# Folding the output parts with one float32 copy and float32 identity matmuls

## The chip, the cores and the metric

The kernel runs on one core of a Trainium2 chip. The metric is the device time of one execution in microseconds, as the median of several runs: 925.74 us before the change (4 runs, 923.92 to 926.63).

## The reference

Two attention layers over the same 2048 tokens of width 512 are computed and mixed by a gate. With g = sigmoid(sum of x * gate_w), the output is g * A + (1 - g) * B.

- A is a recurrent memory transformer with 32 heads of width 128. The tokens come in 64 segments of 32. To each segment 8 memory rows are put in front; q, k and v are projections of these 40 rows, masked softmax attention follows, then the output projection Wo. The first 8 rows of that output are the memory of the next segment, the other 32 are its output rows:

```python
for s in range(n_seg):
    h = concatenate([mem, xs])            # 8 + 32 rows
    ...                                   # q, k, v, softmax, o
    o = einsum('bhte,hed->btd', o, Wo)
    mem = o[:, :M]                        # needed by segment s + 1
    outs.append(o[:, M:])
```

- B is an infini-attention layer with 32 heads of width 16 in 4 blocks of 512 tokens, with a causal mask inside the block and a linear memory over the blocks. It depends on nothing in A.

So the 64 segments of A form a chain: no projection of segment s + 1 can be finished before the Wo product of segment s has become its memory.

## The kernel before

All work is planned in Python as a list of operations for each engine, in a fixed order. A class `Prog` derives the waits from what each operation reads and writes (named resources such as "WH0", and PSUM banks), and `Banks` hands out the eight PSUM banks; which bank an operation gets, and so which earlier reader it must wait for, follows from the order in which banks were given back.

In the first 80 us or so B's projections run and the weights are loaded. Then `plan_a` runs the 64 segments. One segment is a string of units in the order that the list `A_ORDER` (L912) gives, four strings for the four segments of a group. `Q0x` to `V1y` are the projections, `S`, `X`, `M`, `L`, `N` scores and softmax, `PV`, `PL` the product with V, `E` the copies out of PSUM, `W0a` to `W1b` the product with Wo. Between them stand slots for other work: `bS`, `bE`, `bP` for attention B's scores, exponential and product (a share per segment, so that they end around segment 57), `Fc`, `Ff`, `Fe` for fills: projections for the last 8 rows of the coming group's segments (`left_units`), the Wo product of the group's last 8 rows (`ol_units`) and the final mix (`tail_units`).

TensorE is used in four groups of 32 columns: a segment has only 32 rows in the main pass (8 memory rows and 24 of its tokens; the other 8 are handled for four segments at once in the left units), and so each of the four groups takes a part of the heads. For the Wo product this means that a PSUM bank holds, in its four partition strips of 32, four partial sums of the same 32 output rows. They have to be added over the strips and transposed. This is what the fold does: a matmul whose stationary operand is a 128x32 piece of the partial sums and whose moving operand is `fold`, four 32x32 identities on top of each other (128x32), gives the transposed sum.

The partial sums are float32 and the matmul is bf16, so each half (`hf`, 256 columns) of the bank is first split into two bf16 terms:

- H0, H1 (`part_hi`, L1047): copy of the half to `WH` in bf16, on VectorE (DVE).
- l0, l1 (`part_lo`, L1051): `WL` = PSUM - `WH`, in bf16, on DVE. The second gives the PSUM bank back.
- F0, F1 (`fold`, L1058): 16 matmuls each, for two column blocks, two terms (WH and WL accumulate into the same output) and four strips.
- hm0, hm1 copy the first 8 columns, the new memory, to `hT` on ScalarE (ACT); the next segment's Q0x waits for hm0 and Q0y for hm1. ax0, ax1 copy the other 24 to `aT_st` on DVE.

The same two steps and fold serve the Wo product of a group's last rows in `ol_units`, with `LN_sb[:, 0]` and `LN_sb[:, 1]` as the two terms and ACT for the copy. There both halves share one resource name, so that the second copy waits for the first subtraction. For the last group the matmuls are issued in segment 63, and the copies, subtractions and folds come in the final loop (L1453) after the tail units' Wo product of B and its copy `t1` (L1139).

The attention B chain (L867 to L899) turns a bank with a DVE transpose into `oTt` (16 blocks of 32 columns, of which 0 to 15 hold the numerator and 16 the denominator), and writes the reciprocal to `rden`.

Of the kernel before, what the change touches and what calls it, by code (L numbers as in the profile page):

```python
# [5 lines left out]
ALU = mybir.AluOpType  # L6
AX = mybir.AxisListType
BF16 = mybir.dt.bfloat16
F32 = mybir.dt.float32
# [218 lines left out]
def build(nc, es, A_x, A_mem0, A_Wq, A_Wk, A_Wv, A_Wo, B_wq, B_wk, B_wv, B_wo, B_beta, gate_w, out, dbg=None):  # L228
    v = NS()
# [30 lines left out]
    def alloc(stack, *specs):  # L260
        at, spans = 0, {}
        for name, shape, dt, n in specs:
# [14 lines left out]
          ("gBp", [128, 8], F32, 0), ("omgBp", [128, 8], F32, 0),  # L277
          ("onesb", [128, 128], BF16, 0), ("mneg", [128, 224], BF16, 0),
          ("pQj", [128, 512], BF16, 0), ("MZj", [128, 2, 84], BF16, 0), ("PT", [128, 2, 512], BF16, 2), ("orow", [128, 16, 2, 16], BF16, 0),
          ("rden", [128, 16], F32, 0), ("adot", [128, 16, 16], F32, 0),  # L280
          ("oTs", [128, 512], BF16, 0), ("oTg", [128, C, 128], BF16, 0),
          ("KTj", [128, 512], BF16, 2), ("QTj", [128, 512], BF16, 0), ("Vj", [128, 4, 2, 84], BF16, 0),
          ("aTg", [128, C, 128], BF16, 0), ("fold", [128, SEG], BF16, 0), ("VTL", [128, 4, H // 2, 8, 2], BF16, 0),
          ("WH", [128, DM], BF16, 0), ("WL", [128, DM], BF16, 0))
    esP = ExitStack()
    in_p = alloc(esP, ("wkB", [128, C, DM], BF16, 0), ("wqB", [128, C, DM], BF16, 0), ("phK", [128, 4, DM], BF16, 0), ("etmp", [128, 512], BF16, 5),
          ("bmask", [128, 136], BF16, 0), ("mskT", [128, 2, 2, 8, 2], BF16, 0), ("mem0_sb", [128, DM], BF16, 0), ("gwr_sb", [128, 128], BF16, 0), ("beta_sb", [128, HB], BF16, 0),
# [180 lines left out]

def plan_warm(v):
    P, Rs, BK = v.P, v.Rs, v.BK  # L470
    P.op("dve", lambda d: d.memset(v.WH[:, :], 0.0), writes=[Rs("warm")], name="warm0")
    bk = BK.take()

    def f(pe):
        ins = None
        for n in range(WARM):
            ins = pe.matmul(v.pb[bk], v.WH[:, 0:128], v.WH[:, :], start=True, stop=True)
        return ins
    P.op("pe", f, reads=[Rs("warm")], writes=[v.rbank[bk]], name="warm")
    BK.give(bk)  # L480
# [263 lines left out]
class BAttn:  # L744
# [134 lines left out]

    def memory(self, job, G):  # L880
        v, P, Rs = self.v, self.v.P, self.v.Rs
        sb, f = job // 4, job % 4
        nm = "%d_%d%d" % (sb, f, G)
        nb = v.BK.take()

        def fn(pe):
            ins = None
            for j in range(4):
                ins = pe.matmul(v.pb[nb][32 * j:32 * j + 32, :], v.MZj[:, G, 17 * j:17 * j + 32], v.pQj[:, :], start=True, stop=True)
            return ins  # L890
# [3 lines left out]
        rm, rr, rt = v.rden[:, :], Rs("rden"), Rs("oTt")  # L894
# [17 lines left out]
A_ORDER = [o.split() for o in (  # L912
    """
    bT Q0x bE Q0y q0 TQ0 K0x K0y k0 TK0 Q1x bP Q1y q1 K1x TQ1 K1y k1 S0 bS V1x TK1 X0 M0 V0x V0y S1 Ff v0 bE V1y L0 X1 n0 N0 M1 Fe L1 Fc
    PV0 PL0 Fc n1 v1 N1 E0a E0b PV1 PL1 E1a W0a W0b E1b W1a Fe W1b Ff Fe bP H0 bS Fc l0 F0 bP bE hm0 H1 l1 ax0 Fe Ff Fe bS F1 hm1 oL bE
    ax1""",
    """
    Q0x Q0y q0 K0x K0y Q1x k0 Q1y TQ0 TK0 q1 K1x TQ1 K1y S0 X0 V0x V0y k1 M0 V1x TK1 L0 S1 V1y v0 X1 M1 N0 v1 n0 L1 n1 N1 Fc Ff PV0 PL0
    E0b E0a bT Fe Fc PV1 PL1 E1b W0a E1a Fe W0b W1b W1a H0 bP l0 bS H1 Fc F0 bE Ff l1 bP bS hm0 F1 hm1 ax0 oL Fe ax1 bE""",
    """  # L920
    bT Q0x Q0y q0 bP K0x K0y TQ0 k0 TK0 Q1x Q1y K1x K1y S0 q1 bS X0 TQ1 k1 V0x V0y M0 V1x TK1 bE v0 S1 L0 V1y N0 X1 M1 bP n0 L1 PV0 v1 n1
    N1 PL0 E0b PV1 E0a PL1 E1a bP E1b oL bT W0a W0b W1a W1b H0 Fc bS l0 Fc Ff H1 Fe bE l1 Fc F0 Ff Fc F1 hm0 ax0 Fe hm1 ax1 bS bP Fe bE""",
    """
    Q0x Q0y bT q0 K0x K0y k0 TQ0 TK0 Q1x Q1y q1 K1x TQ1 bS K1y S0 bP V0x V0y bE X0 k1 M0 TK1 V1x L0 S1 n0 X1 v0 V1y M1 bP N0 L1 PV0 v1 PL0
    E0b N1 PV1 n1 PL1 E0a bT E1b W0a W0b W1b E1a W1a H0 Ff l0 Fe bS H1 bE oL Ff l1 bS Fe Ff F0 hm0 ax0 Fe F1 hm1 ax1""")]
# [5 lines left out]
def plan_a(v, nseg):  # L931
# [98 lines left out]
        return units  # L1030

    HD = 128 * C // 2
    w_res = (("WH0", "WH1"), ("WL0", "WL1"))
    o_res = (("LN0", "LN0"), ("LN1", "LN1"))

    def out_part(bk, ks, first, lhs, reads, name):

# [6 lines left out]
            return ins  # L1044
        P.op("pe", f, reads=reads + [Rs("Wo%d" % k) for k in sorted({k // 2 for k in ks})], writes=[rbank[bk]], name=name)

    def part_hi(bk, hf, hi, res, name, eng="act"):  # L1047
        c = slice(HD * hf, HD * (hf + 1))
        evac(eng, hi[:, c], pb[bk][:, c], [bk], [Rs(res[0][hf])], "%sh%d" % (name, hf))

    def part_lo(bk, hf, hi, lo, res, name):  # L1051
        c = slice(HD * hf, HD * (hf + 1))
        P.op("dve", lambda d: d.tensor_tensor(lo[:, c], pb[bk][:, c], hi[:, c], ALU.subtract),  # L1053
             reads=[rbank[bk], Rs(res[0][hf])], writes=[Rs(res[1][hf])], name="%sl%d" % (name, hf))
        if hf:
            B.give(bk)

    def fold(bk, hf, hi, lo, res, name):  # L1058

        def f(pe):  # L1060
            ins = None
            for n in range(2):
                for m, t in enumerate((hi, lo)):
                    for j in range(4):
                        o = 256 * hf + 128 * n + SEG * j
                        ins = pe.matmul(pb[bk][SEG * j:SEG * (j + 1), SEG * n:SEG * (n + 1)], t[:, o:o + SEG], v.fold[:, :],  # L1066
                                        start=(m == 0), stop=(m == 1), skip_group_check=True)
# [6 lines left out]
    def ol_units(g):  # L1074
# [5 lines left out]
        for b in range(2):  # L1080
            def u(b=b):
                if b == 0:
                    st["bk"] = B.take()
                out_part(st["bk"], range(4 * b, 4 * b + 4), b == 0, lambda h: OTL[par][:, h, :], [Rs("OTL%d" % par)], "ol%d_%d" % (g, b))
                if b == 1:
                    return u2

            def u2():
                for hf in range(2):
                    part_hi(st["bk"], hf, LN_sb[:, 0, :], o_res, "olev%d" % g)  # L1090
                    part_lo(st["bk"], hf, LN_sb[:, 0, :], LN_sb[:, 1, :], o_res, "olev%d" % g)
            units.append(("c", u, "ol%d_%d" % (g, b)))

        def ut():
            bks = [B.take(), B.take()]
            for hf in range(2):
                fold(bks[hf], hf, LN_sb[:, 0, :], LN_sb[:, 1, :], o_res, "olf%d" % g)
            return lambda: ut2(bks)

        def ut2(bks):  # L1100
# [72 lines left out]
    def segment(s, fill):  # L1173
# [138 lines left out]

        def w_fold(hf):
            wb["f%d" % hf] = B.take()
            fold(wb["f%d" % hf], hf, v.WH, v.WL, w_res, "wf%d" % s)

        def w_mem(hf):
            if s + 1 == nseg:
# [45 lines left out]
        for b in range(2):  # L1364
# [62 lines left out]
    for g in range(ngrp):  # L1427
# [62 lines left out]
```

## Time and profile before

| what | value |
|---|---|
| median of 4 runs | 925.74 us (923.92 to 926.63) |
| the profiled execution | 923.92 us; its span 922.2 us |
| PE (TensorE matmul) busy | 855.2 us, 93% |
| PEld (weight loads) busy | 442.1 us, 48% |
| DVE busy | 651.5 us, 71% |
| ACT busy | 589.2 us, 64% |
| POOL busy | 246.4 us, 27% |
| granted TensorE clock | 0.998 |
| WH copies (DVE, 128) | 53.7 us, 420 ns each |
| WL subtractions (DVE, 128) | 54.4 us, 425 ns each |
| LN subtractions (DVE, 32) | 13.6 us, 425 ns each |

The span runs from the first to the last instruction of the core. Busy times are sums of the records of an engine; a matmul's record includes the time that its data take through the array, so neighbouring records overlap. A row of the groups reads: line, engine, operation, what is written and read, partitions x elements and type, how often; then busy time and mean duration of one; then how long the engine was idle just before such instructions and which instruction ended the idle time. In the chain of work that ended last, each piece has its start and its length, and then the engine, tile and line.

### The profile page before, as it was taken

What the parts mean: (1) busy time and instruction counts of PE and PEld (TensorE: products, weight loads), DVE (VectorE), ACT (ScalarE), POOL (GpSimd) and SP (SyncE); (2) the same over time, 40 slices, a digit from 0 to 9 for tenths busy, and PEclk for the clock granted to TensorE, in tenths of its full rate; (3) what the DMA queues carried; (4) which work ended last, traced back from release to release, by engine and by line L of the source; (5) the groups of instructions that cost most, each with busy time, mean ns of one, the idle gap of its engine ahead of it and who ended that gap; (6) DMA issues with size and microseconds to landing.
All of it is one profiled execution on the core that took longest, in us unless ns stands there. A gap on an engine that the chain in (4) does not pass through costs nothing. (4 is left out here: it accounts for less than half of the span.)

```text
span 922.2 us, 51467 instructions
## 1 busy us (share of the span) xinstructions
PE 855.2 (93%) x23054; PEld 442.1 (48%) x23054; DVE 651.5 (71%) x1507; ACT 589.2 (64%) x1284; POOL 246.4 (27%) x556
## 2 busy tenths in 40 slices
PE   8998989998999999998999999999999989999886
PEld 4544444444444454544454555444444445444443
DVE  3856657776676868677777778777677776868654
ACT  5755666666666666666666666666666666666443
POOL 3601222222222322222233232313222232222110
PEclk9999999999999999999999999999999999999999
DMA  9995000000001111101011111100011111000010
GB/s 324 405 384 188 13 12 17 24 12 24 17 22 43 22 39 33 34 15 27 13 26 38 22 46 32 29 14 22 22 33 38 39 29 38 17 21 5 26 44 20
DMA packets 63957, 51.36 MB, mean 56 GB/s; under 512 B 34288, under 2 KB 60152, under 8 KB 62200
## 3 DMA queue, kind: packets, MB, share of 16 engines
q1 hardware_dynamic: 62008, 35.48, 13.8%
q10 hardware_dynamic: 1728, 12.58, 3.3%
q8 instruction: 181, 2.97, 1.3%
q14 instruction: 40, 0.33, 0.1%
HBM read 33.47 MB, written 14.57 MB: 52 GB/s over the span
## 5 line engine op out<-in xcount | busy, mean ns | idle before, releaser
L816 ACT ACTIVATE PT<-ps 128x1024 bf16<-128x1024 f32 x160 | 163.2, 1020 | 33.9 <-PE ps L802 32.9
L823 POOL TENSOR_SCALAR_AFFINE_SELECT PT<-PT 128x512 bf16<-128x512 bf16 (+1 forms) x96 | 75.5, 787 | 266.5 <-ACT PT L816 256.2
L964 PE MATMUL ps<-Wv_sb,hT 128*32 128x512 bf16 x2048 | 139.3, 379 | 0.0
L964 PE MATMUL ps<-Wq_sb,hT 128*32 128x512 bf16 x2048 | 136.2, 380 | 1.3 <-ACT hT L357 0.8
L964 PE MATMUL ps<-Wk_sb,hT 128*32 128x512 bf16 x2048 | 135.4, 379 | 0.0
L1042 PE MATMUL ps<-Wo_sb,OT_sb 128*32 128x512 bf16 x2048 | 122.3, 380 | 1.3 <-DMA Wo_sb<-in_A_Wo_dram 1.3
L1266 POOL TENSOR_TENSOR P_sb<-P_sb,R_sb 128x64 bf16<-128x64 bf16 x128 | 53.5, 418 | 237.6 <-PE ps L1220 132.7
L357 ACT ACTIVATE OT_sb<-ps 128x320 bf16<-128x320 f32 x192 | 76.7, 434 | 52.3 <-PE ps L1288 38.5
L359 DVE CAST V_sb<-ps 128x512 bf16<-128x512 f32 x128 | 87.7, 685 | 23.9 <-PE ps L964 19.6
L976 DVE STREAM_TRANSPOSE QT_sb<-QN_sb 128x256 f32<-128x256 f32 x128 | 56.3, 440 | 50.9 <-ACT QN_sb L357 50.7
L357 ACT ACTIVATE QN_sb<-ps 128x512 bf16<-128x512 f32 x128 | 77.1, 602 | 21.8 <-PE ps L964 19.0
L964 PEld LDWEIGHTS ps<-Wk_sb,hT 128*32 128x32 bf16 x2048 | 54.0, 97 | 52.7 <-issue 2.3
L359 DVE CAST WH<-ps 128x256 bf16<-128x256 f32 x128 | 53.7, 420 | 33.0 <-PE ps L1042 31.1
L1042 PEld LDWEIGHTS ps<-Wo_sb,OT_sb 128*32 128x32 bf16 x2048 | 50.2, 96 | 46.0 <-issue 1.8
L1229 ACT ACTIVATE P_sb<-ps 128x224 bf16<-128x224 f32 x128 | 45.6, 357 | 40.9 <-PE ps L1220 17.6
L964 PEld LDWEIGHTS ps<-Wq_sb,hT 128*32 128x32 bf16 x2048 | 47.9, 96 | 47.8 <-ACT hT L357 15.3
L976 DVE STREAM_TRANSPOSE KT_sb<-KN_sb 128x256 f32<-128x256 f32 x128 | 56.1, 438 | 15.4 <-ACT KN_sb L357 13.0
L1253 ACT ACTIVATE R_sb<-ps 128x160 f32<-128x160 f32 x128 | 38.9, 304 | 40.4 <-PE ps L1246 40.4
L802 PE MATMUL ps<-QTj,KTj 32*128 32x256 bf16 (+1 forms) x768 | 62.3, 254 | 1.5 <-ACT aT_st L357 1.5
L1260 DVE TENSOR_TENSOR P_sb<-P_sb,R_sb 128x160 bf16<-128x160 bf16 x128 | 42.5, 332 | 29.3 <-ACT R_sb L1256 17.9
L1276 PE MATMUL ps<-P_sb,V_sb 32*128 32x40 bf16 x2048 | 35.3, 178 | 29.9 <-DVE P_sb L1260 13.3
L357 ACT ACTIVATE LN_sb<-ps 128x512 bf16<-128x512 f32 (+1 forms) x96 | 50.5, 526 | 11.8 <-DVE LN_sb L1053 8.8
(136 smaller groups left out, 1549.9 us busy)
## 6 DMA issues: line engine op xcount, KB each, us to landing
Wk_sb<-in_A_Wk_dram ACTq DMA_DIRECT2D x4, 1024.0 KB, 8.4
scr_kqd<-stgk SPq DMA_DIRECT2D x16, 256.0 KB, 8.7
Wq_sb<-in_A_Wq_dram ACTq DMA_DIRECT2D x4, 1024.0 KB, 7.4
Wv_sb<-in_A_Wv_dram ACTq DMA_DIRECT2D x4, 1024.0 KB, 7.5
Wo_sb<-in_A_Wo_dram SPq DMA_DIRECT2D x8, 512.0 KB, 6.8
scr_vd<-V SPq DMA_DIRECT2D x16, 136.0 KB, 6.7
Vj<-scr_vd SPq DMA_DIRECT2D x32, 68.0 KB, 2.4
Wo_sb<-in_A_x_dram SPq DMA_DIRECT2D x8, 256.0 KB, 7.5
```

The costliest lines, as they stand in the source:

```text
L357: P.op("act", lambda a: a.activation(dst, src, ACT.Copy), reads=[v.rbank[k] for k in bks], writes=dres, name=name)
L359: P.op("dve", lambda d: d.tensor_copy(dst, src), reads=[v.rbank[k] for k in bks], writes=dres, name=name)
L802: ins = pe.matmul(v.pb[bks[x]][:, 256 * e + o:256 * e + o + w], KT[e][r, 128 * kc:128 * (kc + 1)], QT[r, q0:q0 + w], start=True, stop=True ...
L816: P.op("act", lambda a: a.activation(pt[:, :, :], v.ps[:, bks[0]:bks[1] + 1, :], ACT.Exp, scale=v.SCALE_B), reads=[v.rbank[b] for b in bks ...
L823: P.op("gp", lambda g: g.affine_select(mv, mv, [[0, mv.shape[1]], [1, 128]], ALU.is_ge, 0.0, base=0, channel_multiplier=-1), reads=[rp], w ...
L964: ins = pe.matmul(pb[bk][SEG * j:SEG * (j + 1), :], lhs(c), cols(w, j) if split else w[:, 512 * j:512 * (j + 1)], start=(c == 0), stop=(c ...
L976: P.op("dve", lambda d: d.transpose(to, src), reads=reads, writes=writes, name=name)
L1042: ins = pe.matmul(pb[bk][SEG * j:SEG * (j + 1), :], lhs(4 * k + j), Wo_sb[:, 4 * k + j, :], start=(first and k == ks[0]), stop=False, skip ...
L1229: P.op("act", lambda a: a.activation(P_sb[:, b, :], pb[bk][:, 0:224], ACT.Exp, scale=SCALE), reads=[rbank[bk]], writes=[Rs("P%d" % b), Rs( ...
L1253: P.op("act", lambda a: a.activation(R_sb[:, b, :], pb[bk][:, 224:384], ACT.Ln), reads=[rbank[bk]], writes=[Rs("R%d" % b)], name="ln%d_%d" ...
L1260: P.op("dve", lambda d: d.tensor_tensor(wide(P_sb, b)[:, :, 0:L], wide(P_sb, b)[:, :, 0:L], R_sb[:, b, :].rearrange("p (i q) -> p i q", q= ...
L1266: P.op(ENG["n"], lambda d: d.tensor_tensor(left(P_sb), left(P_sb), grp04(R_sb[:, b, :]), ALU.mult), reads=[Rs("R%d" % b)], writes=[Rs("P%d ...
```

## The change

The two bf16 terms become one float32 copy, and the fold multiplies it by a float32 `fold` constant: 8 matmuls for each half, each writing its output once, in place of 16 that accumulate in pairs. `part_lo` and the units l0 and l1 disappear. `WF` (float32, 512 columns) takes the room of `WH` and `WL`; in the ol part the two bf16 rows of `LN_sb` are seen as one float32 row, and each half has its own resource. The PSUM bank is given back after the second copy. To make room for the larger `fold`, `rden` goes: the reciprocals are written to the unused column 17 of `oTt`. The copies of the last group's ol part are planned right after the last segment, ahead of the final loop. The matmuls that run at the start to warm TensorE read a bf16 view of `WF`.

```diff
-          ("rden", [128, 16], F32, 0), ("adot", [128, 16, 16], F32, 0),
+          ("adot", [128, 16, 16], F32, 0),
...
-          ("aTg", [128, C, 128], BF16, 0), ("fold", [128, SEG], BF16, 0), ("VTL", [128, 4, H // 2, 8, 2], BF16, 0),
-          ("WH", [128, DM], BF16, 0), ("WL", [128, DM], BF16, 0))
+          ("aTg", [128, C, 128], BF16, 0), ("fold", [128, SEG], F32, 0), ("VTL", [128, 4, H // 2, 8, 2], BF16, 0),
+          ("WF", [128, DM], F32, 0))
...
-    P.op("dve", lambda d: d.memset(v.WH[:, :], 0.0), writes=[Rs("warm")], name="warm0")
+    v.warm = v.WF[:, :].bitcast(BF16)[:, 0:512]
+    P.op("dve", lambda d: d.memset(v.warm[:, :], 0.0), writes=[Rs("warm")], name="warm0")
...
-        rd, rr, rt = v.rden[:, :], Rs("rden"), Rs("oTt")
+        rd, rr, rt = v.oTt[:, :, 17], Rs("oTt"), Rs("oTt")
...
-    PV0 PL0 Fc n1 v1 N1 E0a E0b PV1 PL1 E1a W0a W0b E1b W1a Fe W1b Ff Fe bP H0 bS Fc l0 F0 bP bE hm0 H1 l1 ax0 Fe Ff Fe bS F1 hm1 oL bE
+    PV0 PL0 Fc n1 v1 N1 E0a E0b PV1 PL1 E1a W0a W0b E1b W1a Fe W1b Ff Fe bP H0 bS Fc F0 bP bE hm0 H1 ax0 Fe Ff Fe bS F1 hm1 oL bE
...
-    w_res = (("WH0", "WH1"), ("WL0", "WL1"))
-    o_res = (("LN0", "LN0"), ("LN1", "LN1"))
+    LNF = LN_sb[:, :, :].rearrange("p a d -> p (a d)").bitcast(F32)
...
-    def part_hi(bk, hf, hi, res, name, eng="act"):
+    def part_out(bk, hf, dst, res, name, eng="act"):
         c = slice(HD * hf, HD * (hf + 1))
-        evac(eng, hi[:, c], pb[bk][:, c], [bk], [Rs(res[0][hf])], "%sh%d" % (name, hf))
-
-    def part_lo(bk, hf, hi, lo, res, name):
-        c = slice(HD * hf, HD * (hf + 1))
-        P.op("dve", lambda d: d.tensor_tensor(lo[:, c], pb[bk][:, c], hi[:, c], ALU.subtract),
-             reads=[rbank[bk], Rs(res[0][hf])], writes=[Rs(res[1][hf])], name="%sl%d" % (name, hf))
+        evac(eng, dst[:, c], pb[bk][:, c], [bk], [Rs(res % hf)], "%sh%d" % (name, hf))
         if hf:
             B.give(bk)
 
-    def fold(bk, hf, hi, lo, res, name):
+    def fold(bk, hf, part, res, name):
 
         def f(pe):
             ins = None
             for n in range(2):
-                for m, t in enumerate((hi, lo)):
-                    for j in range(4):
-                        o = 256 * hf + 128 * n + SEG * j
-                        ins = pe.matmul(pb[bk][SEG * j:SEG * (j + 1), SEG * n:SEG * (n + 1)], t[:, o:o + SEG], v.fold[:, :],
-                                        start=(m == 0), stop=(m == 1), skip_group_check=True)
+                for j in range(4):
+                    o = 256 * hf + 128 * n + SEG * j
+                    ins = pe.matmul(pb[bk][SEG * j:SEG * (j + 1), SEG * n:SEG * (n + 1)], part[:, o:o + SEG], v.fold[:, :],
+                                    start=True, stop=True, skip_group_check=True)
             return ins
-        P.op("pe", f, reads=[Rs(res[0][hf]), Rs(res[1][hf]), Rs("fold")], writes=[rbank[bk]], name="%s_%d" % (name, hf))
+        P.op("pe", f, reads=[Rs(res % hf), Rs("fold")], writes=[rbank[bk]], name="%s_%d" % (name, hf))
...
                 for hf in range(2):
-                    part_hi(st["bk"], hf, LN_sb[:, 0, :], o_res, "olev%d" % g)
-                    part_lo(st["bk"], hf, LN_sb[:, 0, :], LN_sb[:, 1, :], o_res, "olev%d" % g)
+                    part_out(st["bk"], hf, LNF, "LN%d", "olev%d" % g)
...
-            units["H%d" % b] = lambda b=b: part_hi(wb["bk"], b, v.WH, w_res, "wev%d" % s, ENG["H%d" % b])
-            units["l%d" % b] = lambda b=b: part_lo(wb["bk"], b, v.WH, v.WL, w_res, "wev%d" % s)
+            units["H%d" % b] = lambda b=b: part_out(wb["bk"], b, v.WF, "WF%d", "wev%d" % s, ENG["H%d" % b])
...
         rest = ended or ol_units(g)
+    if ended:
+        whole(ended[0])
+        rest = ended[1:]
     if nseg == 64:
```

l0 and l1 leave the other three strings of `A_ORDER` in the same way, and `memory` writes its reciprocal to column 17 of `oTt` as `chain` does.

More of the change, by code (lines that the diff above doesn't have):

```diff
@@ L476, in f @@
         for n in range(WARM):
-            ins = pe.matmul(v.pb[bk], v.WH[:, 0:128], v.WH[:, :], start=True, stop=True)
+            ins = pe.matmul(v.pb[bk], v.warm[:, 0:128], v.warm[:, :], start=True, stop=True)
         return ins
@@ L893, in memory @@
         self.load(job + 1, G, "v")
-        rm, rr, rt = v.rden[:, :], Rs("rden"), Rs("oTt")
+        rm, rr, rt = v.oTt[:, :, 17], Rs("oTt"), Rs("oTt")
         P.op("dve", lambda d: d.tensor_scalar(rm, den, 1e-6, None, op0=ALU.add), reads=[rt, rr], writes=[rr], name="bdm" + nm)
@@ L918 @@
     Q0x Q0y q0 K0x K0y Q1x k0 Q1y TQ0 TK0 q1 K1x TQ1 K1y S0 X0 V0x V0y k1 M0 V1x TK1 L0 S1 V1y v0 X1 M1 N0 v1 n0 L1 n1 N1 Fc Ff PV0 PL0
-    E0b E0a bT Fe Fc PV1 PL1 E1b W0a E1a Fe W0b W1b W1a H0 bP l0 bS H1 Fc F0 bE Ff l1 bP bS hm0 F1 hm1 ax0 oL Fe ax1 bE""",
+    E0b E0a bT Fe Fc PV1 PL1 E1b W0a E1a Fe W0b W1b W1a H0 bP bS H1 Fc F0 bE Ff bP bS hm0 F1 hm1 ax0 oL Fe ax1 bE""",
     """
     bT Q0x Q0y q0 bP K0x K0y TQ0 k0 TK0 Q1x Q1y K1x K1y S0 q1 bS X0 TQ1 k1 V0x V0y M0 V1x TK1 bE v0 S1 L0 V1y N0 X1 M1 bP n0 L1 PV0 v1 n1
-    N1 PL0 E0b PV1 E0a PL1 E1a bP E1b oL bT W0a W0b W1a W1b H0 Fc bS l0 Fc Ff H1 Fe bE l1 Fc F0 Ff Fc F1 hm0 ax0 Fe hm1 ax1 bS bP Fe bE""",
+    N1 PL0 E0b PV1 E0a PL1 E1a bP E1b oL bT W0a W0b W1a W1b H0 Fc bS Fc Ff H1 Fe bE Fc F0 Ff Fc F1 hm0 ax0 Fe hm1 ax1 bS bP Fe bE""",
     """
     Q0x Q0y bT q0 K0x K0y k0 TQ0 TK0 Q1x Q1y q1 K1x TQ1 bS K1y S0 bP V0x V0y bE X0 k1 M0 TK1 V1x L0 S1 n0 X1 v0 V1y M1 bP N0 L1 PV0 v1 PL0
-    E0b N1 PV1 n1 PL1 E0a bT E1b W0a W0b W1b E1a W1a H0 Ff l0 Fe bS H1 bE oL Ff l1 bS Fe Ff F0 hm0 ax0 Fe F1 hm1 ax1""")]
+    E0b N1 PV1 n1 PL1 E0a bT E1b W0a W0b W1b E1a W1a H0 Ff Fe bS H1 bE oL Ff bS Fe Ff F0 hm0 ax0 Fe F1 hm1 ax1""")]
 A_ENG = dict(E0a="dve", E0b="act", E1a="act", E1b="act", H0="dve", H1="dve", K0="act", K1="dve", KL0="dve", KL1="act", OL="act",
@@ L1096, in ut @@
             for hf in range(2):
-                fold(bks[hf], hf, LN_sb[:, 0, :], LN_sb[:, 1, :], o_res, "olf%d" % g)
+                fold(bks[hf], hf, LNF, "LN%d", "olf%d" % g)
             return lambda: ut2(bks)
@@ L1314, in w_fold @@
             wb["f%d" % hf] = B.take()
-            fold(wb["f%d" % hf], hf, v.WH, v.WL, w_res, "wf%d" % s)
+            fold(wb["f%d" % hf], hf, v.WF, "WF%d", "wf%d" % s)
         def w_mem(hf):
```

## The prediction

> **What bounds the kernel now.** I read the page first: busy times, slices, granted clock.
>
> ```profile
> PE 855.2 (93%) x23054; PEld 442.1 (48%) x23054; DVE 651.5 (71%) x1507; ACT 589.2 (64%) x1284; POOL 246.4 (27%) x556
> PEclk9999999999999999999999999999999999999999
> ```
>
> TensorE (PE) is the engine with the most work, at full clock throughout, so what it is given costs time unless it fills a gap. "93%" flatters it, since a matmul's record includes its way through the array: a 32-column matmul shows 0.176 us, yet groups of four follow each other every 0.025 to 0.03 us. So next came the groups by line with shapes kept apart, for the instructions that the change touches (mean ns of one; then the engine's idle time before them).
>
> ```profile
> L1053 DVE TENSOR_TENSOR WL<-ps,WH 128x256 bf16<-128x256 f32 x128 | 54.4, 425 | 4.4
> L359 DVE CAST WH<-ps 128x256 bf16<-128x256 f32 x128 | 53.7, 420 | 33.0 <-PE ps L1042 31.1
> L1066 PE MATMUL ps<-fold,WH 128*32 128x32 bf16 x1024 | 30.5, 180 | 9.4 <-DVE WL L1053 4.6 <-ACT hT L357 3.3 <-DVE aT_st L359 0.9
> L1066 PE MATMUL ps<-fold,WL 128*32 128x32 bf16 x1024 | 29.9, 176 | 0.0
> L1053 DVE TENSOR_TENSOR LN_sb<-ps,LN_sb 128x256 bf16<-128x256 f32 x32 | 13.6, 425 | 13.0 <-ACT LN_sb L357 12.1
> ```
>
> The subtractions (the l steps) take 160 x 0.425 = 68 us of DVE, which is not the engine with the most work. They matter where PE waits for them. The timeline shows one fold of the middle as PE sees it:
>
> ```profile
> 410.77 0.19 PE L1066 MATMUL ps<-fold,WH 128*32 128x32 bf16 x4
> 410.80 0.19 PE L1066 MATMUL ps<-fold,WL 128*32 128x32 bf16 x4
> 410.82 0.19 PE L1066 MATMUL ps<-fold,WH 128*32 128x32 bf16 x4
> 410.85 0.19 PE L1066 MATMUL ps<-fold,WL 128*32 128x32 bf16 x4
> 410.87 0.28 PE L849 MATMUL ps<-PT,Vj 128*32 128x256 bf16 x4
> ```
>
> A fold of 16 bf16 matmuls holds PE for 0.10 to 0.11 us: four column groups work at once. Last I read the chain that ended last, near its end, where attention B has run out and nothing fills PE:
>
> ```profile
> 899.12 0.44 DVE WH L359
> ...
> 899.58 0.43 DVE WL L1053
> 900.01 0.34 DVE WH L359
> ...
> 900.37 0.43 DVE WL L1053
> ...
> 900.85 0.28 PE ps L1066 x16
> ```
>
> Here the four DVE steps stand on the path one behind the other. To price the whole I went through the timeline from 84 us on, took 0.166 us (0.176 less 0.01 of streaming) off each PE record's end, and summed the gaps ahead of folds: 10.8 us before 856 us (48 gaps), 5.6 us after it (10), 3.8 us ahead of the two last folds of an LN part. Part of the 10.8 is listed under ACT hT, but those folds begin about 0.1 us after their second subtraction ends (438.05 after 437.92): they too wait for WL.
>
> **What the Trainium skill says.** FP8 and Floating Point Precision, TensorE Precision Notes: true float32 takes four passes through the array (high and low halves of both operands). Nothing here shows it; the kernel has only bf16 matmuls. TensorE: Matmul & The Clock Gate, LDWEIGHTS: a weight load takes columns / 1.2 ns, 26.7 ns for 32; the cadence above agrees, so a fold is bound by weight loads, not by the 32 columns it streams. The same page, The mechanism: matmuls on different column or row tiles overlap; the four per 0.027 us agree. Perfetto Trace Analysis, Engine Utilization, halves the array's output rate for FP32_LOW_HIGH, which reads as two halves per matmul; no run shows it.
>
> **The change part by part.**
>
> Removed: 128 WL and 32 LN subtractions. F0 (first fold) now needs H0 alone, F1 needs H1. H1 follows H0 directly on DVE, so H0 is 0.42 us of work, H1 another 0.41, and F1's data are ready about 0.83 us earlier: before, WH starts at 861.06 and F1 at 862.78; after, 861.06 + 0.42 + 0.41 + about 0.06 of handing over = 861.95. What is late next: PE itself in the middle; hm (0.18 us on ACT) and the next Q pass in the tail.
> - Middle: of 10.8 us I take back 9; some F0 still meet H1 or a PSUM bank that is read late.
> - Tail, folds at 862, 876, 888, 900: 4 x 0.83 = 3.3 us. At 912 the first fold stands behind 32 Wo matmuls (issued 910.73, with 1.90 us of records), so 0.2 us.
> - LN parts: the two ACT copies no longer wait for the subtraction between them. For the last group they also move ahead of t1: LN's ACT copy starts at 915.83 now, the fold at 917.64, ACT's aT copy at 917.99. Afterwards the fold can run behind L1133 (about 915.1) and the aT copy behind t1, which ends at 915.83: 2.2 us.
> Sum of the gain: 9 + 3.3 + 0.2 + 2.2 = 14.7 us; ceiling 10.8 + 5.6 + 3.8 = 20, and up to 3 more if DVE's relief (68 of 651 us) or ACT's (8.8 us idle for LN's subtraction) hastens other copies. I count nothing for that: DVE is not late at the steps where PE waits longest (L1276, 40 us of gaps, behind softmax).
>
> Neutral: H0/H1 and LN copies write float32 in place of bf16. Nearest rows: DVE's transpose to float32 706 ns against 685 for a cast to bf16 of equal shape, so at most 3% of 54 us, 1.6 us of DVE, hidden by PE; without that cover about 0.02 us per fold. The reciprocals (254 ns) write a strided column of oTt instead of rden: same engine, same count, 56 x perhaps 0.02 us, hidden by PE. fold's constant and the warm view run while PE has its projections. Banks come free at H1 rather than l1: some bS, K and Q take others, whose readers have long finished; zero, with 1 us either way. No DMA and no SP or POOL step moves.
>
> Added: 160 folds (128 W, 32 LN) of 8 float32 matmuls in place of 16 bf16 ones. No row shows one, so bounds:
> - Low: two half loads per matmul, 16 as now, column groups overlapping as now: 0.107 us, nothing added. A gain here has no reason: the loads are not fewer.
> - Four loads per matmul, still overlapping: 32 x 27 / 4 = 0.215 us, +0.11.
> - Taken: two half loads, which lie in the *same* column group and so cannot overlap each other, while the neighbour overlaps partly: per matmul from 27 + 4 (the start-to-start of neighbouring tiles that The mechanism gives) to 54 ns, middle 43; 8 x 43 = 0.34 us, +0.235. I take it since today's overlap rests on neighbouring matmuls going to different groups, and a low and a high half of one matmul do not.
> - High: four passes in a row, 8 x 4 x 27 = 0.86 us, +0.755.
> Behind the fold on PE wait the fills and the next segment's projections; PE goes straight on with them, so the extra counts in full, except F0 in the five tail segments, which hides behind H1: 160 x 0.235 - 5 x 0.235 = 36.4 us.
>
> Sum: 36.4 - 14.7 = +21.7 us. On the profiled execution, 923.92 us (span 922.2 and 1.7 around it), that is 945.6; it stands 1.8 below the median 925.74, so the forecast is 947 us. Break-even is a fold of 0.107 + 14.7 / 160 = 0.20 us.
>
> **The rivals.**
> - A, faster: the four column groups stay concurrent in float32 and the fold takes 0.107 to 0.215 us: 925.7 - 14.7 = 911 up to 925.7 + 17 - 14.7 = 928. For it: the pages know column tiling and float32 without a word against both together, and a fold is load-bound, so extra streaming may hide under loads. Against: the neighbouring halves. It decides below 0.20 us.
> - C, PE becomes far dearer: four passes in a row, 0.86 us: 160 x 0.755 = 121, less 14.7 and about 2 hidden in the tail: 1030. For it: four passes is what the page states; against: the halved rate on the other.
> - D: each half waits until the one before it has drained, 16 x 0.176 = 2.8 us a fold: 430 us more, about 1340. Nothing in the profile asks for it.
> - That the wait merely moves (F1 held by its bank's reader rather than by WL) would cost at most the 9 us of the middle and lies inside B's range.
>
> **How the numbers follow.** A 0.33, B (the forecast, folds of 0.25 to 0.45 us, 933 to 965 us) 0.40, C 0.20, D 0.07. The 0.2% (1.9 us) that a measurement of this kernel can just tell cuts a piece off A: faster 0.27, the same 0.06, slower 0.67. The range runs from 908 (A with most of the 20 us ceiling) to 1031 (C): outside lie D, C's upper side (0.06) and 0.05 below.
>
> **What would show it.** Each step has its place. The WL rows are gone, F1 starts within 0.1 us of H1 in the tail, the gaps ahead of folds fall from 20 us to under 6; the last LN copies stand before t1. A fold's first matmul to the next PE instruction reads 0.34 us: 0.11 says A, 0.86 says C. If the fold is cheap and the time still does not fall, the gaps ahead of folds went elsewhere and my 14.7 is wrong; if folds take 0.34 and the time rises by less, PE has slack that I count as none.

## The result and the profile after

The changed kernel takes 922.87 us (median of 35 runs, 920.13 to 931.87, and a single one at 3456, which is left aside) against 925.19 us of the kernel before beside it (56 runs): ratio 0.9985, 95% interval 0.9972 to 0.9997. That is 1.4 us less (0.3 to 2.6; the medians alone lie 2.3 us apart), on the edge of what a measurement of this kernel can tell from no change. The forecast was 947 us, slower. The profiled execution of after took 924.83 us, its span 923.1 us.

The page, its first line:

```profile
PE 860.8 (93%) x23054; PEld 450.6 (49%) x23054; DVE 586.6 (64%) x1347; ACT 590.3 (64%) x1284; POOL 246.5 (27%) x556
```

DVE lost its 160 subtractions (1507 to 1347 instructions) and 65 us of work, ACT and POOL nothing. The number of PE instructions has not moved: a float32 matmul leaves *two* weight loads and *two* matmul records, so 8 of them leave the 16 that 16 bf16 matmuls left. PE has 5.6 us more of busy time.

The groups of after by line with shapes kept apart (busy, mean ns; then PE's or DVE's idle time just before them, and who ended it):

```profile
L965 PE MATMUL ps<-Wq_sb,hT 128*32 128x512 bf16 x2048 | 136.6, 380 | 4.0 <-ACT hT L357 3.4 <-DVE aT_st L359 0.6
L359 DVE COPY WF<-ps 128x256 f32<-128x256 f32 x128 | 48.4, 420 | 36.3 <-PE ps L1042 34.4
L1060 PE MATMUL ps<-fold,WF 128*32 128x32 f32 x2048 | 37.5, 198 | 2.4 <-DVE WF L359 1.3 <-DVE aT_st L359 0.3
L1060 PE MATMUL ps<-fold,LN_sb 128*32 128x32 f32 x512 | 7.6, 199 | 0.7 <-ACT t_sb L1132 0.7
L850 PE MATMUL ps<-PT,Vj 128*32 128x256 bf16 x512 | 36.5, 275 | 1.1 <-DMA MZj<-scr_mzd 1.1
```

Of before, the row of the Q projection:

```profile
L964 PE MATMUL ps<-Wq_sb,hT 128*32 128x512 bf16 x2048 | 136.2, 380 | 1.3 <-ACT hT L357 0.8
```

Idle time ahead of the folds fell from 9.4 + 3.4 us to 2.4 + 0.7. But the next segment's Q projection, which had 1.3 us of idle time before it, now has 4.0. A copy to float32 takes the 420 ns that the cast to bf16 took. The last row of after holds one wait, at 757 us, for a load of `MZj`, an operand of attention B, that landed late; it is needed in the sums below.

PE's timeline in the middle, two folds (start, length, engine, line):

```profile
413.00 0.30 PE L1060 MATMUL ps<-fold,WF 128*32 128x32 f32 x16
413.12 0.28 PE L850 MATMUL ps<-PT,Vj 128*32 128x256 bf16 x4
...
413.66 0.33 PE L1060 MATMUL ps<-fold,WF 128*32 128x32 f32 x16
413.80 0.40 PE L890 MATMUL ps<-pQj,MZj 128*32 128x512 bf16 x4
```

The next PE instruction starts 0.12 and 0.14 us after the fold's first. Over all folds the median of this is 0.147 us, against 0.114 us before: 0.033 us more, where I had put 0.235.

**Where the time went, by stage.** PE executes nearly the same list in all these kernels. I matched the PE instructions of two traces in order and compared how long each stage takes. The stages are the middle (84 to 853 us, attention B still running or just ended) and the tail (from 853 us on, nothing left to fill PE). In some profiles TensorE's granted clock drops for about 3.4 us (after: 0.88 and 0.69 in two stretches of 4 us at 756), 1.7 us of lost clock each; what of it lies inside a stage is taken off. (In e4, e6, e9, e11 and e12 one such drop lies around the first fold, and only the part behind the start of the middle counts.) Loads that land late are left in: PE waits for one in after (1.1 us), e4, e5, e8 and e10 (0.4 to 0.8 us, all between 755 and 761 us) and e9 (2.6 us, at 345), and for none in before. This differs between executions of one kernel: e4 has 0.5 us of it, e11 none. The first 84 us, work that ends before the first fold, differ by up to 7.6 us from one profile to the next and are left out. The last column is the distance of the measured ratio from 1, times 925.5 us.

| kernel, against before | middle, us | tail, us | sum | from the ratio, us |
|---|---|---|---|---|
| the change | +3.5 | -5.3 | -1.8 | -1.4 (-2.6 to -0.3) |
| e1, every fold twice | +22.8 | -1.8 | +21.0 | +22.8 (+19.6 to +25.9) |
| e2, one bf16 term | -7.9 | -5.3 | -13.3 | -11.2 (-14.2 to -8.3) |
| e3, moved end alone | 0.0 | -2.3 | -2.3 | -1.7 (-3.3 to 0) |
| e4, bank returned late | +0.7 | -5.5 | -4.8 | -6.3 (-8.2 to -4.3) |
| e5, folds early | -2.0 | -5.7 | -7.8 | -6.8 (-9.4 to -4.3) |
| e6, both | +4.7 | -5.9 | -1.2 | -0.6 (-2.0 to +0.6) |
| e7, loops exchanged | +6.3 | -5.1 | +1.2 | +1.9 (-0.3 to +4.1) |
| e8, e4 with idle subtractions | +1.5 | -3.7 | -2.2 | -2.1 (-3.9 to -0.5) |
| e9, e5 with a later return | +2.8 | -5.2 | -2.4 | -4.3 (-6.1 to -2.6) |
| e10, late in the fourth string | +2.4 | -5.3 | -2.9 | -2.5 (-4.1 to -0.9) |
| e11, e4 again | +0.7 | -5.5 | -4.8 | -5.2 (-7.7 to -2.8) |
| e12, e8 again | +0.5 | -3.7 | -3.2 | -1.7 (-3.8 to +0.6) |

The sums by stage lie inside the intervals of the timed runs, but for e9, which comes to -5.0 without its late load of 2.6 us; so the stages can be read, to about 1 us. The change lost 3.5 us in the middle, 1.1 of them at the late load, and won 5.3 us in the tail.

### The profile page after: what moved, and what is told of

It is laid out like the page before. It is cut to its first block, busy times and chain, and to the rows that moved or that the text cites. A ratio compares the mean times of both kernels' runs of the same rounds, so it can differ in the third digit from the quotient of the medians.

```text
span 923.1 us, 51314 instructions
## 1 busy us (share of the span) xinstructions
PE 860.8 (93%) x23054; PEld 450.6 (49%) x23054; DVE 586.6 (64%) x1347; ACT 590.3 (64%) x1284; POOL 246.5 (27%) x556
## 5 line engine op out<-in xcount | busy, mean ns | idle before, releaser
L817 ACT ACTIVATE PT<-ps 128x1024 bf16<-128x1024 f32 x160 | 163.8, 1024 | 34.8 <-PE ps L803 33.0
L359 DVE CAST aT_st<-ps 128x48 bf16<-128x48 f32 x129 | 25.7, 199 | 81.2 <-ACT hT L357 76.3
L965 PEld LDWEIGHTS ps<-Wq_sb,hT 128*32 128x32 bf16 x2048 | 50.2, 97 | 49.1 <-ACT hT L357 16.5
L359 DVE COPY WF<-ps 128x256 f32<-128x256 f32 x128 | 48.4, 420 | 36.3 <-PE ps L1042 34.4
L803 PE MATMUL ps<-QTj,KTj 32*128 32x256 bf16 (+1 forms) x768 | 62.5, 255 | 1.7 <-ACT PT L817 0.6
```

The lines of the kernel that those rows point to most:

```text
L359: P.op("dve", lambda d: d.tensor_copy(dst, src), reads=[v.rbank[k] for k in bks], writes=dres, name=name)
L803: ins = pe.matmul(v.pb[bks[x]][:, 256 * e + o:256 * e + o + w], KT[e][r, 128 * kc:128 * (kc + 1)], QT[r, q0:q0 + w], start=True, stop=True ...
L817: P.op("act", lambda a: a.activation(pt[:, :, :], v.ps[:, bks[0]:bks[1] + 1, :], ACT.Exp, scale=v.SCALE_B), reads=[v.rbank[b] for b in bks ...
L965: ins = pe.matmul(pb[bk][SEG * j:SEG * (j + 1), :], lhs(c), cols(w, j) if split else w[:, 512 * j:512 * (j + 1)], start=(c == 0), stop=(c ...
```

## The experiments

My theory before them: the fold is cheap, the tail gave what was forecast, and the middle kept almost nothing of its 9 us, because F1's wait had turned into other waits. The rival: the fold costs the forecast's order of time, hidden under something.

**e1, every fold twice: what does a fold cost?**

```diff
-            for n in range(2):
-                for j in range(4):
+            for _ in range(2):
+                for n in range(2):
+                    for j in range(4):
```

> The changed kernel with every float32 fold done twice over (the same 8 matmuls again into the same columns; the output stays the same). In the changed kernel a fold holds PE for 0.12 to 0.15 us (first matmul to next instruction, median 0.147). If PE time at a fold counts in full, as my sum took it, 160 x 0.12 to 0.147 = 19 to 23 us more than the changed kernel, near 943. If a fold's extra is absorbed in waits that follow it (rival: PE waits for hm or for a bank anyway), clearly less than half of it, under 10 us.

947.66 us (4 runs; before 925.45), ratio 1.0246 (1.0212 to 1.028). In the traces it is 22.8 us longer than the change, by the ratios 24.1 us: 0.14 to 0.15 us for each of the 160 added folds, at the upper end of what was expected or a little above. PE's timeline of e1, a doubled fold:

```profile
421.87 0.46 PE L1061 MATMUL ps<-fold,WF 128*32 128x32 f32 x32
422.15 0.41 PE L890 MATMUL ps<-pQj,MZj 128*32 128x512 bf16 x4
```

0.28 us to the next instruction, against 0.14 us for the same pair in after (413.66, 413.80). The second fold adds 0.128 us in the median. So hardly anything hides an added fold: PE time counts in full, and the fold is as cheap as its records say.

**e2, one bf16 term.** The fold reads a bf16 copy of the partial sums with a bf16 `fold`; the low-order term of the split is left out.

```diff
-          ("aTg", [128, C, 128], BF16, 0), ("fold", [128, SEG], F32, 0), ("VTL", [128, 4, H // 2, 8, 2], BF16, 0),
-          ("WF", [128, DM], F32, 0))
+          ("aTg", [128, C, 128], BF16, 0), ("fold", [128, SEG], BF16, 0), ("VTL", [128, 4, H // 2, 8, 2], BF16, 0),
+          ("WF", [128, DM], BF16, 0))
...
-    LNF = LN_sb[:, :, :].rearrange("p a d -> p (a d)").bitcast(F32)
+    LNF = LN_sb[:, 0, :]
```

> The changed kernel with the copy and the fold constant in bf16: 8 bf16 matmuls per fold, no subtraction; the low-order term of the split is left out, so the sums are those of bf16 parts. This is the changed kernel with the cheapest possible fold. By the same full count: a fold of about half of 0.114 us, 0.05 to 0.06, so 0.09 less for each of 160, about 14 us under the changed kernel, near 909. If the wait of the third segment string has merely moved behind the folds (PE now waits for hm0), the fold's price is hidden there (32 folds) and the gain is 10 us or less.

914.12 us, ratio 0.9879 (0.9847 to 0.991). Eight bf16 matmuls hold PE for 0.064 us in the median. Against the change the middle is 11.4 us shorter, and 0.147 - 0.064 = 0.083 us on the 148 folds of the middle gives 12.3 us; the tail is the same. The 14 us that I had expected do not come. Of the 11.4, 1.1 are the late load of after, which e2 does not have, and in e2's groups the Q pass waits 5.1 us and B's scores 2.9 us, against 4.0 and 1.7 in after: some 2 us of the fold's price are hidden by waits behind it. So the new schedule would take 914 us with a fold of 0.064 us, and what the float32 fold costs beyond that is paid in the middle.

**e3, the moved end alone.** The kernel before, with the last copies planned ahead of the final loop.

```diff
         rest = ended or ol_units(g)
+    if ended:
+        whole(ended[0])
+        rest = ended[1:]
```

> The kernel before with only the early copies of the last group's ol part (they and their subtractions stand ahead of the final loop), all else bf16 in two terms. My sum gave this move 2.2 us of the tail: expected 1.5 to 2.5 us under the kernel before (-0.16 to -0.27%). Rival: it is the absence of the two subtractions there that shortens the tail, and then the move alone gives under 1 us, since copies and subtractions alternate for 1.75 us and end later than t1.

923.52 us (22 runs), ratio 0.9982 (0.9964 to 1.0). The middle of this trace and of the one before differ by 0.02 us in all, the tail by -2.27 us (forecast: 2.2). The timeline of e3 near its end:

```profile
913.58 0.38 ACT L357 ACTIVATE LN_sb<-ps 128x256 bf16<-128x256 f32 x1 [2.78 <-PE ps L1042]
...
915.54 0.68 ACT L1139 ACTIVATE t_sb<-ps,omg_sb 128x512 f32<-128x512 f32 x1
...
916.25 0.38 PE L1066 MATMUL ps<-fold,LN_sb 128*32 128x32 bf16 x32 [0.90 <-ACT t_sb L1139]
```

The copy to `LN_sb` now stands ahead of t1 on ACT; before, it began at 915.73 behind it. This move alone is as large as the whole change's -1.8. The float32 fold in itself, the rest of the change, comes out at +0.5 us in the traces, or -0.6 without the late load: no gain that these runs can tell.

**e4 and e11, the bank returned late: what do the earlier returns do?** In the change the bank of the Wo product goes back at H1. Here it goes back where l1 stood, in all four strings.

```diff
-        if hf:
+        if hf and give:
             B.give(bk)
...
+            units["l%d" % b] = lambda b=b: b and B.give(wb["bk"])
...
-    E0b N1 PV1 n1 PL1 E0a bT E1b W0a W0b W1b E1a W1a H0 Ff Fe bS H1 bE oL Ff bS Fe Ff F0 hm0 ax0 Fe F1 hm1 ax1
+    E0b N1 PV1 n1 PL1 E0a bT E1b W0a W0b W1b E1a W1a H0 Ff l0 Fe bS H1 bE oL Ff l1 bS Fe Ff F0 hm0 ax0 Fe F1 hm1 ax1
```

> The changed kernel with the Wo bank given back at the place in the plan where the second subtraction stood, so that every later operation gets the bank it had in the kernel before; no instruction is added. In the changed kernel's trace six folds wait behind t1's bank (1.8 us together) and 28 score matmuls of B behind H1's bank (1.3 us together). If those waits are the cost of the new bank order, 2 to 3 us under the changed kernel. If they only move to another engine's chain, no difference (within 1 us).

919.32 us (6 runs), ratio 0.9932 (0.9911 to 0.9953): the only edit is who gets which bank, and it is 3.0 us faster than the change in the traces (about 1 us of it in the one segment where after has the late load and the drop of the clock), 4.9 by the ratios. Run once more on another chip:

> The kernel of e4 once more, beside the next one on one chip. Theory: 918.5 to 920.5 us. If it reads 922 or more, what e4 showed belonged to its chip.

921.55 us (19 runs), ratio 0.9944 (0.9917 to 0.997), with before at 925.70 beside it. That lies above the 918.5 to 920.5 us that I had written and below the 922 that would have undone it: the two intervals overlap over most of their length, and e4's six runs were on the low side. The two traces agree within 0.1 us in the middle. Part of it has a name: in the change the folds of six segments took a bank that t1, ACT's copy of the gate's matmuls, was still reading. These waits are 1.5 us between 84 and 745 us and 0.3 us after that, and they are gone in e4. The other wait that I had named, of B's score matmuls, is not: their idle time is 1.7 us in after and 1.6 in e4.

**e10, late in the fourth string only.** All those segments have the fourth string; the give is put back there alone.

```diff
-    E0b N1 PV1 n1 PL1 E0a bT E1b W0a W0b W1b E1a W1a H0 Ff Fe bS H1 bE oL Ff bS Fe Ff F0 hm0 ax0 Fe F1 hm1 ax1
+    E0b N1 PV1 n1 PL1 E0a bT E1b W0a W0b W1b E1a W1a H0 Ff Fe bS H1 bE oL Ff g bS Fe Ff F0 hm0 ax0 Fe F1 hm1 ax1
+            units["g"] = lambda: B.give(wb["bk"])
```

> The changed kernel with the Wo bank given back at the old place (where l1 stood) in the fourth string alone; the other three strings as in the change. Theory (the folds that wait for t1 stand in fourth strings only, and they are what e4 won back): as e4, 918.5 to 920.5 us. Rival (e4's gain came from banks of the other strings): as the change, 922 to 924 us.

922.09 us (22 runs), ratio 0.9973 (0.9956 to 0.999). The t1 waits are gone to the last hundredth (-1.51 and -0.31 us in the same places), but the middle is only 1.1 us shorter than the change's, not 2.8 (e4, e11). So the rival holds: the t1 waits are the smaller part of what e4 wins. The groups of e10, and those of e4 and e11 in the same way, show why so little is left of them:

```profile
L1060 PE MATMUL ps<-fold,WF 128*32 128x32 f32 x2048 | 38.9, 198 | 4.9 <-ACT PT L817 3.2 <-DVE WF L359 1.3 <-DVE aT_st L359 0.4
```

F1 of the fourth strings now waits, 3.2 us in all, for a bank that the exponential (L817) still reads, while the Q pass, with 4.0 us of idle time in the change, has 1.6: again a wait that moved. Compared segment by segment, without the one with the late load, the middle is shorter than the change's by 1.7 us in e4, 1.6 in e11 and 0.65 in e10. The fourth strings give 0.5 us in all three; the second give 1.0 in e4 and e11 and 0.3 in e10, the first 0.3 and 0.1. So most of the rest comes with the banks of the second string; which wait there is the cause stays open.

**e5, the fourth string's folds early.** With l0 and l1 gone, F0 needs only H0. In this string it still stood far behind.

```diff
-    E0b N1 PV1 n1 PL1 E0a bT E1b W0a W0b W1b E1a W1a H0 Ff Fe bS H1 bE oL Ff bS Fe Ff F0 hm0 ax0 Fe F1 hm1 ax1
+    E0b N1 PV1 n1 PL1 E0a bT E1b W0a W0b W1b E1a W1a H0 Ff Fe bS F0 hm0 H1 F1 hm1 ax0 ax1 bE oL Ff bS Fe Ff Fe
```

> The changed kernel with the fourth segment string reordered: F0 and hm0 directly after the first score slot, then H1, F1, hm1, ax0, ax1, and only then attention B's exponential and the other fills. In the changed kernel's trace F0 and F1 of that string lie together (0.147 us apart) and PE then waits some 0.5 us until hm0 has gone through ACT, where it stands behind an exponential of 1.02 us. If that is where the gain of the middle went, 16 strings x 0.3 to 0.5 us = 5 to 7 us under the changed kernel. Rival: the exponential now starts later and PE waits for it at the next product of B, then under 2 us or slower.

918.87 us (8 runs; before 925.76), ratio 0.9926 (0.9898 to 0.9954): the best of these kernels with the full float32 sums, 5.5 us under the change in the traces' middle. Segment by segment, without the one with the late load, it is 4.4 us, 4.0 of them in the fourth strings. The groups of e5:

```profile
L965 PE MATMUL ps<-Wq_sb,hT 128*32 128x512 bf16 x2048 | 136.4, 380 | 0.9 <-ACT hT L357 0.5
L803 PE MATMUL ps<-QTj,KTj 32*128 32x256 bf16 x512 | 50.0, 273 | 0.8 <-ACT PT L817 0.6
L1060 PE MATMUL ps<-fold,WF 128*32 128x32 f32 x2048 | 38.7, 198 | 1.7 <-DVE WF L359 1.4
```

The wait of the Q pass for the memory copy (hT), 3.4 us in the change, is 0.5 here: hm0 now goes to ACT ahead of B's exponential.

**e6, e4 and e5 together.** The edit is e5's order with l0 and l1 of e4 as late returns.

> The same reordering on the kernel with the bank given back late (e4, 919.3 us). If both effects are independent, another 4 to 7 us less than e4, 912 to 915, and this is the fastest of all with the full float32 sums. If the reordering only replaces the bank waits, the same as e4.

925.39 us (22 runs), ratio 0.9993 (0.9978 to 1.0007). The two gains do not add; both go, and the middle is 6.7 us longer than e5's. The groups of e6, the two rows that grew:

```profile
L803 PE MATMUL ps<-QTj,KTj 32*128 32x256 bf16 x512 | 50.2, 273 | 5.9 <-DVE aT_st L359 4.1 <-ACT hT L357 1.2 <-ACT PT L817 0.6
L1126 PE MATMUL ps<-woB_sb,oTg 128*32 128x512 bf16 x256 | 16.7, 379 | 2.1 <-ACT hT L357 2.1
```

B's scores (L803) and the gate's matmuls (L1126) now get banks that the fold's readers, the copies to hT and aT_st, have only just read: 5.9 + 2.1 us of waits, 0.8 and 0.0 in e5.

**e9, e5 with the return after F1 in the fourth string.** By the plan this keeps t1 away from the folds and gives the gate's matmuls a bank read long before. The edit is shown against e5; its unit `g` is that of e10.

```diff
-    E0b N1 PV1 n1 PL1 E0a bT E1b W0a W0b W1b E1a W1a H0 Ff Fe bS F0 hm0 H1 F1 hm1 ax0 ax1 bE oL Ff bS Fe Ff Fe
+    E0b N1 PV1 n1 PL1 E0a bT E1b W0a W0b W1b E1a W1a H0 Ff Fe bS F0 hm0 H1 F1 g hm1 ax0 ax1 bE oL Ff bS Fe Ff Fe
```

> The changed kernel with the fourth string's folds early as in e5, and the Wo bank of that string given back after F1 instead of after H1. By the plan the folds then wait for no t1 copy, and the bank of the gate's row matmuls (brow) is again one that an aT copy read last, as in e4, where these matmuls did not wait. Theory (it is the bank order that took e5's 2.6 us at brow and ruined e6): 2 to 3 us below e5, about 916 us, ratio to the kernel before 0.987 to 0.992. Rival (the early folds and a late return of the bank do not go together, as e6 suggested): 922 to 926 us.

921.33 us (22 runs), ratio 0.9953 (0.9934 to 0.9972): 2.5 us above e5, so my theory failed, and so did the rival. Its premise fails too: e5's groups list no idle time at the gate's matmuls (0.0), where I had put 2.6 us. The groups of e9 say who pays:

```profile
L803 PE MATMUL ps<-QTj,KTj 32*128 32x256 bf16 x512 | 50.2, 274 | 3.6 <-ACT hT L357 3.0 <-ACT PT L817 0.6
```

The gate's matmuls wait for no ACT copy any more (one of them, in this execution, waits 2.6 us for a transfer that landed late). But B's scores, first in line after the fold, now get the bank that hm reads: 3.0 us. I had looked at two users of the banks and moved the wait to a third.

**e7, the fold's loops exchanged: must two float32 matmuls of one strip wait for each other?** The strip j outside, the column block n inside, so that four records in a row go to the same 32 columns of TensorE.

```diff
-            for n in range(2):
-                for j in range(4):
+            for j in range(4):
+                for n in range(2):
```

> The changed kernel with the two loops of the fold exchanged, so that the two matmuls of one strip (one column group) follow each other; same 8 matmuls. My forecast took the two halves of a float32 matmul as serial because they share a column group, which the trace does not bear out (0.147 us a fold). If matmuls of one column group cannot overlap, the fold becomes 0.2 to 0.3 us and the kernel 8 to 25 us slower than the changed one; if the queue overlaps them whatever their order, no change within 2 us.

928.44 us (12 runs), ratio 1.0021 (0.9997 to 1.0044). In the change the records start in groups of four, about 4 ns apart, with some 20 ns between the groups; here they start mostly about 13 ns apart, and a fold takes 0.15 us or a little more. The middle is 2.8 us longer, 0.019 us per fold: between the two expectations, and far nearer to the second. Four groups at once are slightly better, but records of one strip do not stand in a row behind each other either: 16 of them at 27 ns would be 0.43 us.

**e8 and e12, idle subtractions: what is DVE's relief worth?** The 128 subtractions of the W parts are put back into e4 as work that nobody uses: each writes its half of the PSUM bank once more.

```diff
+        def sub_again(hf):
+            c = slice(HD * hf, HD * (hf + 1))
+            P.op("dve", lambda d: d.tensor_tensor(pb[wb["bk"]][:, c], pb[wb["bk"]][:, c], v.WF[:, c], ALU.subtract),
+                 reads=[rbank[wb["bk"]], Rs("WF%d" % hf)], writes=[rbank[wb["bk"]]], name="wev%dl%d" % (s, hf))
+            if hf:
+                B.give(wb["bk"])
...
-            units["l%d" % b] = lambda b=b: b and B.give(wb["bk"])
+            units["l%d" % b] = lambda b=b: sub_again(b)
```

> The kernel e4 with the 128 W subtractions put back on DVE as idle work: same place in the order, the result overwrites the PSUM half and nothing reads it, the folds do not wait for it. It measures what relieving DVE of 128 x 0.425 = 54 us is worth by itself, with the bank free as late as in the kernel before. If the relief is worth nothing, as my sum took it, e4's time within 1 us, apart from the tail, where H1 again stands behind the first subtraction (4 x 0.43 = 1.7 us): 919 to 921. If DVE's queue matters in the middle too, 3 us or more above e4.

> The kernel of e8 once more (e4 with the 128 W subtractions as idle work on VectorE, whose result nobody reads), beside e4 on one chip. Theory (the relief of VectorE is worth nothing before the tail and 1.7 us in it): 1.5 to 2.5 us above e11. Rival (the relief counts in the middle too): 4 us or more above e11. Nothing of it at all: within 0.5 us of e11.

e8 reads 923.67 us (20 runs), ratio 0.9977 (0.9958 to 0.9995); e12 923.89 us (14 runs), ratio 0.9982 (0.9959 to 1.0006), 2.3 us above e11 on the same chip. In the traces the tail is 1.8 us longer both times. The chain that ended last, in e12:

```profile
902.36 0.44 DVE WF L359
902.82 0.45 DVE ps L1308
903.28 0.44 DVE WF L359
903.76 0.33 PE ps L1060 x16
```

The idle subtraction (L1308) stands between H0 and H1 and holds up F1. In the middle e8 is 0.9 us above e4 and e12 0.2 us below e11: DVE's relief is worth between nothing and 1 us there. (The medians of e8 and e4 lie 4.4 us apart, which by e8's expectation would have spoken for the middle; the pair on one chip, e11 and e12, does not repeat it.)

## Why the prediction was wrong, step by step

**The fold's price: the step that failed.** "Taken: two half loads, which lie in the *same* column group and so cannot overlap each other", 0.34 us a fold, +0.235. Measured: 0.147 us, +0.033; times 148 folds 4.9 us in the middle in place of some 35. The two halves are there, as two load and two matmul records for each float32 matmul (loads 113 ns against 93 in bf16, matmuls 196 against 176). That they cannot overlap was my own addition, and e7 speaks against it. The Trainium skill came near the number, and I weakened it: Perfetto Trace Analysis, Engine Utilization, says that FP32_LOW_HIGH halves the output rate. Here a fold of 8 float32 matmuls holds PE for 0.147 us and one of 8 bf16 matmuls for 0.064 us (e2), a factor of 2.3. Of the four passes in FP8 and Floating Point Precision, TensorE Precision Notes, the records show two, and nothing of the price of four. The overlap of column groups in TensorE: Matmul & The Clock Gate, The mechanism, holds for float32 as for bf16: in after too the records of four strips start about 4 ns apart. So a fold in float32 costs what the two bf16 terms cost, plus about 0.03 us. That is rival A, near its low end (0.107 to 0.215 us), and A's time, 911 to 928 us, holds the result.

**The gain of the middle: 9 us taken, 1.4 to 2.5 kept** (the +3.5 measured, with or without the late load of 1.1 us, less 4.9 for the folds). With the measured fold my own sum would have been 925.7 + 160 x 0.033 - 14.7 = 916.3 us. It is 922.87: that is the part of the miss that the fold does not explain. The prediction's own last sign, a cheap fold and a time that still does not fall, is what came. I wrote that folds listed under hT "too wait for WL", and that is how it was; the mistake was to count a wait as gain without asking who waits for what beside it. The timeline of before at such a place:

```profile
436.87 1.02 ACT L816 ACTIVATE PT<-ps 128x1024 bf16<-128x1024 f32 x1
...
437.50 0.42 DVE L1053 TENSOR_TENSOR WL<-ps,WH 128x256 bf16<-128x256 f32 x1
437.79 0.18 ACT L357 ACTIVATE hT<-ps 128x16 bf16<-128x16 f32 x1
...
438.08 0.20 PE L1066 MATMUL ps<-fold,WH 128*32 128x32 bf16 x4 [0.53 <-ACT hT L357]
...
438.18 1.09 PE L964 MATMUL ps<-Wq_sb,hT 128*32 128x512 bf16 x16
```

and of after, at the same place:

```profile
439.10 1.02 ACT L817 ACTIVATE PT<-ps 128x1024 bf16<-128x1024 f32 x1
...
439.46 0.46 PE L1060 MATMUL ps<-fold,WF 128*32 128x32 f32 x32
440.02 0.26 ACT L357 ACTIVATE hT<-ps 128x16 bf16<-128x16 f32 x2
...
440.25 1.05 PE L965 MATMUL ps<-Wq_sb,hT 128*32 128x512 bf16 x16 [0.33 <-ACT hT L357]
```

Before, two waits ran side by side: F1 for WL until 437.92, and hm0 on ACT, behind an exponential of 1.02 us, until 437.79. Afterwards F0 and F1 go through together (x32), and Q waits for hm0, which ends no sooner. In nine of the 15 fourth strings with a Q pass behind them F1 came more than 0.5 us after F0 before; in the other six it followed at once (0.103 us). Where it had come after 0.807 us, it typically comes after 0.147 now, and F1 to Q rose from 0.103 to 0.644 us: of 0.66 us saved 0.54 came back. Over all 15, F0 to F1 fell by 5.1 us and F1 to Q rose by 4.2. I named the wait that "merely moves" as a rival, but looked for it at F1's bank and not one instruction further.

The prediction's own measure has a flaw besides. By it the idle time ahead of folds in the middle fell from 10.8 to 5.8 us (with the tail 9.0 are left, where its sign was a fall from 20 to under 6). But 30 of the 48 gaps of before, 2.9 us in all, are just under 0.1 us each, with no releaser in the profile; after has 37 of them, 3.6 us. They were never the subtractions' to give. Another 1.8 us of the 5.8 are the six folds that wait for t1. In the whole middle: idle time ahead of folds -5.0 us; Q's idle time in the groups, 1.3 to 4.0, +2.7; the folds themselves +4.9; the late load +1.1. That is +3.7 us where the traces have +3.5. e5 is the counterproof: it sends hm0 ahead of the exponential, and 4.0 us come in the fourth strings.

**Banks: "zero, with 1 us either way".** Wrong by its size. The order of returns alone moved the kernel by 3.0 us in the traces (e4) and took 6.7 us of middle from e5 (e6 against e5). "Whose readers have long finished" was not so for the folds that got t1's bank.

**The tail: right.** Forecast 3.3 + 0.2 + 2.2 = 5.7 us, less what the fold costs there; measured 5.3, and the 12 folds of the tail cost 12 x 0.033 = 0.4. F1 follows H1 at once in after's chain:

```profile
891.80 0.44 DVE WF L359
892.28 0.33 PE ps L1060 x16
```

and e12 puts 1.8 us of it on the subtractions alone. The end move was forecast at 2.2 us, and e3 measured 2.27. (The prediction has LN's copy of before start at 915.83; that is t1's end, and the copy starts at 915.73. The 2.2 us rest on t1's end and stand.) The timeline of after shows the copy ahead of t1 as the prediction asked, and where the next limit lies:

```profile
916.42 0.66 ACT L357 ACTIVATE LN_sb<-ps 128x256 f32<-128x256 f32 x2 [2.78 <-PE ps L1042]
...
918.14 0.69 ACT L1132 ACTIVATE t_sb<-ps,omg_sb 128x512 f32<-128x512 f32 x1 [1.06 <-PE ps L1126]
918.73 0.21 ACT L357 ACTIVATE aT_st<-ps 128x64 bf16<-128x64 f32 x1
918.88 0.33 PE L1060 MATMUL ps<-fold,LN_sb 128*32 128x32 f32 x16 [0.72 <-ACT t_sb L1132]
```

The second LN fold waits for t1's bank. Had it come right behind the first (0.15 us), it would have started about 0.87 us earlier.

**DVE's relief, "I count nothing for that"**: borne out within 1 us in the middle (e8, e12); it counts where H1 stands behind l0, in the tail. The float32 copies at the price of the bf16 casts: right (420 ns both). The reciprocals in a column of oTt: 257 ns against 254.

## What to carry to other kernels

When a wait is taken away, follow the chain past the instruction that is freed: what it frees is worth only the difference to the next wait that already runs beside it, and the way to collect the rest is to move that one too (e5). A split into two bf16 terms for a small, column-tiled matmul was replaced here by float32 at nearly the same TensorE time (0.147 us a fold against 0.114), but nothing is won by it where the split was hidden. Where buffers are handed out in order of their return, moving a return by two steps is an edit of its own, worth 3 to 7 us here, and it has to be tried for each schedule, since two good edits together can be worth nothing (e6).

## What the runs showed that I had not expected

- A float32 matmul with a 128x32 stationary piece and 32 moving columns leaves two load and two matmul records; eight of them, on four column groups, hold PE for 0.147 us when they stand alone and 0.128 us more when doubled; eight bf16 ones hold it for 0.064 us, sixteen for 0.114.
- Records that follow each other on the same 32 columns (e7) start mostly about 13 ns apart, half the 27 ns that I had taken as the least distance.
- Which PSUM bank an operation gets moved this kernel by up to 6.5 us with the same instructions in the same order on PE (change against e4, e5 against e9 and e6).
